# Dilated-window attention and MLP, two layers on one core: chunk products added on DVE, weights spread by DMA, stages reordered, first layernorm transposed on PE

## The chip, the cores, the metric

The kernel runs on 1 core of a Trainium2 chip. The metric is device time in microseconds (us), median of several executions. Engines: PE does the matmuls, DVE is the vector engine, ACT the scalar engine, POOL is GpSimd, SP issues most of the DMAs. Most executions of one kernel agree within about 0.3% (1350.36 to 1353.33 us before the change). Some fall into a slower state, and are not compared. They show a lower granted PE clock: the share of PE's full speed that the chip allowed, 1.00 being all of it.

## The reference

```python
def _A_ref(x, wqkv, wo):            # H = 32 heads of 32, window W = 8, dilation 2
    qkv = x @ wqkv                  # S = 2048, D = 1024
    # position s attends to s, s-2, ..., s-14 (masked where negative)
    logits = einsum("bhsd,bhswd->bhsw", q, kg) * Dh ** -0.5
    attn = softmax(where(mask, logits, -1e9), axis=-1)
    o = einsum("bhsw,bhswd->bhsd", attn, vg)
    return o.reshape(B, S, D) @ wo

def _B_ref(x, w1, b1, w2, b2):      # F = 3584
    return gelu(x @ w1 + b1) @ w2 + b2

x = A_x
for layer in range(2):              # written out in the original
    x = x + _A_ref(_layernorm(x), A_wqkv, A_wo)
    x = x + _B_ref(_layernorm(x), B_w1, B_b1, B_w2, B_b2)
```

All in bf16, with f32 sums in PSUM.

## The kernel before

The sequence is cut into 4 groups of 512 positions; with 2 layers that makes 8 units of work, "groups 0 to 7". A group passes the stages qkv (24 chunks of 8 matmuls, 128x128 weights against 512 columns), wo (8 chunks), ffn1 (28 chunks of 8) and ffn2 (32 rows of 7): 704 main matmuls. The attention sits between them on DVE, with PE helping in two places: the head sums (sum of q*k over the 32 values of a head, by a 0/1 matrix) and the spread of the attention weights from 32 rows per block to 128 partitions.

Names in the profiles: `wt` is a tile of weights, `xn` the layernorm of x and `xnT` its transpose, `qT`, `kT` and `vT` the outputs of qkv, `big` a product on DVE, `L` the head sums, `a` the attention weights and `abc` the same after the spread, `oT` the output of the attention, `hT` that of ffn1, `tmp` a step of the sum into x, and `acc` a buffer in PSUM, where the matmuls write. "av" multiplies the spread weights by v and adds over the window.

```python
wpool = ctx.enter_context(tc.tile_pool(name="wpool", bufs=6))   # 1 MB weight tiles
...
def mm(*args, **kwargs):                  # PE keeps the order of the program
    inst = nc.tensor.matmul(*args, **kwargs)
    if last_pe[0] is not None:
        dep_order(inst, last_pe[0], "PE program order")
    ...
def ln_tile(t, tt, xnT):
    ...                                   # bn_stats, bn_aggr on DVE, rstd on POOL
    nc.vector.tensor_scalar(out=xn[:], in0=x[t][:], scalar1=mv[:, 0:1], scalar2=rstd[:], ...)
    nc.sync.dma_start_transpose(xnT[:, tt, :, :], xn[:].rearrange("s (k p) -> s k p", p=P))

def gen_qkv(n):
    ...
    def reduce_one():                     # head sum of one chunk: 8 matmuls on PE
        c, prod = pend.pop(0)
        for wh in range(2):
            for tb in range(NTT):
                mm(L[tb*H:(tb+1)*H, wh*4:(wh+1)*4, :], lhsT=smat[:], rhs=prod[...],
                   start=(c == 0), stop=(c == NCH - 1), tile_position=(0, tb * H))
        if c == NCH - 1:
            ...                           # mask
            softmax(s, L)
    for c in range(NCH):                  # k chunks
        ps = qkv_chunk(wk, c, xnT)
        nc.scalar.copy(kT[:, c, HALO:], ps[:])
        nc.vector.tensor_tensor(out=prod[:], in0=qT[...], in1=win(kT[:, c, :]), op=ALU.mult)
        pend.append((c, prod))
        if len(pend) > 2:
            reduce_one()
    ...                                   # v chunks, with the last reduce_one()s

def spread(n):                            # 8 matmuls and 8 ACT copies
    for wh in range(2):
        for tb in range(NTT):
            mm(ps[:], lhsT=selbc[...], rhs=a[...], tile_position=(tb * H, 0))
            nc.scalar.copy(abc[...], ps[...])

def av(n, c):                             # one chunk: multiply, then add over the window
    nc.vector.tensor_tensor(out=pv[:], in0=abc, in1=win(vT[:, c, :]), op=ALU.mult)
    ...                                   # three adds, 2048, 1024 and 512 columns

# order of the stages
mk_ln_a(0); run(gen_qkv(0), ...)
run(gen_qkv(1), {1: spread(0), 2 + c: av(0, c), 12: layernorm of 2})
run(gen_wo(0))
for n in range(1, N):
    run(gen_ffn1(n - 1), {1: spread(n), 2 + 3 * c: av(n, c)})
    # last n: wo(n), ffn2(n-1), ffn1(n), ffn2(n); otherwise:
    run(gen_ffn2(n - 1), {8: layernorm of n + 1}); run(gen_wo(n)); run(gen_qkv(n + 1))
```

## Time and profile before

| | before |
|---|---|
| time, median of 4 | 1351.88 us |
| span of the profile | 1350.7 us |
| PE busy | 1285.6 us, 95% |
| head-sum matmuls on PE | 512 |
| first main matmul | 24.8 us |

The first fence is the page of the kernel before; the columns of an engine are busy us, share of the span, and number of instructions.

```profile
span 1350.7 us, 14693 instructions
PE 1285.6 (95%) x6222; PEld 628.1 (46%) x6222; DVE 722.0 (53%) x809; ACT 329.3 (24%) x530; POOL 56.0 (4%) x158
```

PE is the bound, but 95% busy doesn't say what a busy microsecond does. The chain of waits of the same kernel does (start in us, duration in us, engine, what it wrote, source line, number of instructions):

```profile
340.38 0.69 ACT hT L308
341.07 1.46 ACT abc L261 x3
342.57 126.21 PE acc L87 x584
468.77 0.55 PE L L87 x8
469.32 1.88 PE acc L87 x8
471.20 0.55 PE L L87 x8
...
500.31 0.69 ACT hT L308
```

584 matmuls in 126.21 us are 216.1 ns each. From one head-sum block to the next (468.77 to 471.20) 2.43 us pass, while 8 main matmuls need 1.73 us: a block costs PE 0.70 us, though it shows as 0.55. From 340.38 to 500.31 one group takes 159.93 us; its 704 main matmuls need 152.1.

What PE itself waited for, all of the run (engine, line, releaser: us in total, times, longest):

```profile
PE acc L87 <- DMA xnT<-xn: 31.8, 2, 24.8
PE L L87 <- DVE big L220: 24.6, 4, 14.7
PE acc L87 <- ACT hT L308: 1.7, 7, 0.2
```

All the large waits lie before 183 us. The timeline shows the one at the start (start, duration, engine, operation, count; in brackets the idle time before it and its releaser):

```profile
10.03 6.10 SPq L151 DMA_TRANSPOSE xnT<-xn  x2
18.17 4.50 SPq L151 DMA_TRANSPOSE xnT<-xn  x2
24.78 20.77 PE L87 MATMUL acc<-xnT,wt 128*128 128x512 bf16 x88 [24.78 <-DMA xnT<-xn]
```

And a window (start:end, length, then busy us of each engine, then the granted PE clock) shows PE starved by DVE in the av chain of group 0, with the clock down:

```profile
115.00:130.00 15.00, 7.51 (x40) 2.86 (x39) 15.00 (x12) 1.17 (x2) 0.00 (x0) 0.73 0.00 0
```

DVE is busy for all of the 15 us, PE for half of them, at a clock of 0.73.

### The profile page before, as it was taken

The numbers are of one execution on the slowest core, as the hardware profiler recorded it, in microseconds if no ns is written. First come the engines' busy times: TensorE is split into PE (matmuls) and PEld (weight loads), VectorE is DVE, ScalarE is ACT, GpSimd is POOL, SyncE is SP. The second block draws the span as 40 slices with busy tenths as digits, with TensorE's granted clock in tenths as the row PEclk, the third lists the DMA queues.
The fourth block names the chain that finished last, engine by engine and source line by source line (L and its number), as shares of the span: only waits on it lengthen the run. The fifth ranks groups of instructions, "written<-read, shape, count | busy, mean of one in ns | idle before, by whom it ended". The sixth has DMA issues, their size and how long they took to land.

```text
span 1350.7 us, 14693 instructions
## 1 busy us (share of the span) xinstructions
PE 1285.6 (95%) x6222; PEld 628.1 (46%) x6222; DVE 722.0 (53%) x809; ACT 329.3 (24%) x530; POOL 56.0 (4%) x158
## 2 busy tenths in 40 slices
PE   2893979999999999999999999999999999999998
PEld 1461534455444554445544454445544455444443
DVE  3669754177723759147571666417782455932003
ACT  1240233013520254102540035201441024400310
POOL 3100000010000100001000100001000000000000
PEclk9896989999999999999999999999999999999999
DMA  9740554554645544555645545456464654466440
GB/s 257 212 163 15 157 145 139 168 156 126 197 145 169 174 140 148 155 159 147 183 140 175 166 147 171 145 170 178 132 183 145 206 167 127 147 173 198 154 137 31
DMA packets 218976, 210.93 MB, mean 156 GB/s; under 512 B 71392, under 2 KB 190176, under 8 KB 216864
## 3 DMA queue, kind: packets, MB, share of 16 engines
q1 hardware_dynamic: 218752, 209.74, 51.3%
q8 instruction: 48, 0.79, 0.2%
q0 software_dynamic: 160, 0.27, 0.2%
q14 instruction: 16, 0.13, 0.0%
HBM read 189.01 MB, written 4.19 MB: 143 GB/s over the span
## 4 chain that ended last, share of the span: by engine, by line
PE 90%; DVE 4%; ACT 2%; DMA 1%; issue 0%; POOL 0%; SPq 0%; DVEq 0%; ACTq 0%
PE acc L87 87%; PE L L87 3%; DVE big L268 1%; ACT abc L261 1%; DVE big L269 1%; DVE big L220 0%; DVE stats L143 0%; DMA xnT<-xn 0%; ACT hT L308 0%; DVE big L270 0%; DMA x_93<-in_A_x_dram 0%; DVE xn L150 0%; SPq L151 0%; POOL rstd L148 0%; DVE oT L271 0%
## 5 line engine op out<-in xcount | busy, mean ns | idle before, releaser
L87 PE MATMUL acc<-xnT,wt 128*128 128x512 bf16 x3328 | 743.0, 383 | 32.7 <-DMA xnT<-xn 31.8
L87 PEld LDWEIGHTS <-wt 128*128 128x128 bf16 x3328 | 391.5, 120 | 383.4 <-issue 67.0
L87 PE MATMUL acc<-wt,hT 128*128 128x512 bf16 x1792 | 388.1, 379 | 0.0
L87 PEld LDWEIGHTS <-hT 128*128 128x128 bf16 x1792 | 175.3, 98 | 211.4
L327 DVE TENSOR_TENSOR tmp<-acc,b2bc 128x512 f32<-128x512 f32 x64 | 44.3, 692 | 393.9 <-PE acc L87 389.5
L308 ACT ACTIVATE hT<-acc,b1T 128x512 bf16<-128x512 f32 x224 | 154.3, 690 | 285.2 <-PE acc L87 285.1
L220 DVE TENSOR_TENSOR big<-qT,kT 128x4096 bf16<-128x4096 bf16 x64 | 143.0, 2286 | 44.6 <-ACT kT L218 43.7
L268 DVE TENSOR_TENSOR big<-abc,vT 128x4096 bf16<-128x4096 bf16 x64 | 143.7, 2285 | 28.9 <-ACT abc L261 28.9
L194 ACT CAST qT<-acc 128x512 bf16<-128x512 f32 x64 | 37.6, 587 | 465.3 <-PE acc L87 465.3
L87 PE MATMUL acc<-wt,oT 128*128 128x512 bf16 x512 | 111.8, 379 | 0.0
L87 PEld LDWEIGHTS <-oT 128*128 128x128 bf16 x512 | 50.1, 98 | 60.3
L269 DVE TENSOR_TENSOR big<-big 128x2048 bf16<-128x2048 bf16 x64 | 75.4, 1218 | 0.0
L218 ACT CAST kT<-acc 128x512 bf16<-128x512 f32 x64 | 37.5, 586 | 132.4 <-PE acc L87 132.4
L87 PE MATMUL L<-big,smat 128*32 128x512 bf16 x512 | 41.2, 399 | 24.6 <-DVE big L220 24.6
L147 POOL TENSOR_TENSOR rstd<-mv,eps_t 128x1 f32<-128x1 f32 x64 | 14.6, 231 | 1143.5 <-DVE mv L145 1143.5
L232 ACT CAST vT<-acc 128x512 bf16<-128x512 f32 x64 | 37.4, 584 | 70.0 <-PE acc L87 69.8
L270 DVE TENSOR_TENSOR big<-big 128x1024 bf16<-128x1024 bf16 x64 | 41.3, 685 | 0.0
L148 POOL TENSOR_TENSOR rstd<-rstd,mhalf 128x1 f32<-128x1 f32 x64 | 35.7, 561 | 4.1
L261 ACT CAST abc<-acc 128x512 bf16<-128x512 f32 x64 | 32.0, 629 | 0.0
L87 PEld LDWEIGHTS <-smat 128*32 128x32 bf16 x512 | 8.2, 95 | 49.7 <-issue 49.7
L241 DVE TENSOR_REDUCE mx<-L 128x128 f32<-128x1024 f32 x8 | 9.7, 1218 | 29.9 <-PE L L87 29.9
L246 DVE TENSOR_REDUCE z<-e 128x128 f32<-128x1024 f32 x8 | 15.7, 1964 | 16.5 <-ACT e L244 16.5
(102 smaller groups left out, 331.6 us busy)
## 6 DMA issues: line engine op xcount, KB each, us to landing
wt<-in_B_w_dram SPq DMA_DIRECT2D x56, 1024.0 KB, 5.6
wt<-in_B_w_dram SPq DMA_DIRECT2D x64, 896.0 KB, 4.8
wt<-in_A_wqkv_dram SPq DMA_DIRECT2D x48, 1024.0 KB, 5.4
wt<-in_A_wo_dram SPq DMA_DIRECT2D x16, 1024.0 KB, 4.9
xnT<-xn SPq DMA_TRANSPOSE x64, 4.2
x_85<-in_A_x_dram SPq DMA_DIRECT2D x1, 256.0 KB, 2.8
x_86<-in_A_x_dram SPq DMA_DIRECT2D x1, 256.0 KB, 3.1
x_87<-in_A_x_dram SPq DMA_DIRECT2D x1, 256.0 KB, 4.1
```

Of the source, the lines that this page charges most:

```text
L87: inst = nc.tensor.matmul(*args, **kwargs)
L148: nc.gpsimd.tensor_tensor(out=rstd[:], in0=rstd[:], in1=mhalf[:], op=ALU.pow)
L194: nc.scalar.copy(qT[:, c, :], ps[:])
L218: nc.scalar.copy(kT[:, c, HALO:], ps[:])
L220: nc.vector.tensor_tensor(out=prod[:], in0=qT[:, c, :].unsqueeze(1).to_broadcast([P, W, T]), in1=win(kT[:, c, :]), op=ALU.mult)
L232: nc.scalar.copy(vT[:, c, HALO:], ps[:])
L261: nc.scalar.copy(abc[:, wh * 4:(wh + 1) * 4, tb * P:(tb + 1) * P], ps[:].rearrange("p (w t) -> p w t", w=4))
L268: nc.vector.tensor_tensor(out=pv[:], in0=s["abc"][:], in1=win(s["vT"][:, c, :]), op=ALU.mult)
L269: nc.vector.tensor_tensor(out=pv[:, 0:4, :], in0=pv[:, 0:4, :], in1=pv[:, 4:8, :], op=ALU.add)
L270: nc.vector.tensor_tensor(out=pv[:, 0:2, :], in0=pv[:, 0:2, :], in1=pv[:, 2:4, :], op=ALU.add)
L308: nc.scalar.activation(hT[:, j, :], ps[:], ACT.Gelu_apprx_tanh, bias=b1T[:, j:j + 1])
L327: nc.vector.tensor_tensor(out=tmp[:], in0=pss[tt][:], in1=b2bc[:, dh * HALF:(dh + 1) * HALF], op=ALU.add)
```

## The change

The intent is to leave PE only main matmuls, and to keep it fed from the start on:

1. In groups 2 to 7, the 8 products are added on DVE (7 adds in a tree), and PE sums heads once instead of 8 times. The head sum moved into `attend`, 5 chunks into the following ffn1.
2. In groups 2 to 6 the weights are spread by DMA through DRAM: 4 DMAs out, 4 back.
3. The first layernorm is transposed on PE, with warm-up matmuls around it.
4. qkv(1) and two thirds of qkv(2) come ahead of wo(0), and the wo stages of groups 1 and 7 are put inside ffn2 of the group before, after 4 of its 32 rows. The layernorms of groups 1 and 2 are scaled on ACT.

To pay for the memory there are 5 weight buffers instead of 6. Smaller changes go with it: the order of instructions is pinned on POOL, and on DVE in the first layernorm; x and the weights are loaded in another order; the constants are built later; and the first six q chunks of qkv(0) run in two halves, so that they can start with half of the weights.

```diff
-    wpool = ctx.enter_context(tc.tile_pool(name="wpool", bufs=6))
+    wpool = ctx.enter_context(tc.tile_pool(name="wpool", bufs=5))
+    dram = ctx.enter_context(tc.tile_pool(name="dram", bufs=2, space=bass.MemoryType.DRAM))
...
+    vec, act, pool, sp = InOrder(nc.vector), InOrder(nc.scalar), InOrder(nc.gpsimd), InOrder(nc.sync)
...
+    def ln_first():
+        ...
+            for k in range(KD):
+                pe(nc.tensor.transpose(pst[:, k, :], xn[:, k * P:(k + 1) * P], ident[:]))
+            act.copy(xa[0][:, tt, :, :], pst[:])
+            warm_up(4)
...
+    def new_prod(n, c):
+        vec.tensor_tensor(out=prod[:], in0=qT..., in1=win(kT...), op=ALU.mult)
+        tree.append(prod)
+        if s["on_pe"]:
+            if len(tree) > 2:
+                head_sum(n, tree.pop(0), False)
+        elif c % 2 == 1:
+            for _ in range(min(2, len(tree) - 1)):
+                b = tree.pop()
+                vec.tensor_tensor(out=tree[-1][:], in0=tree[-1][:], in1=b[:], op=ALU.add)
...
+        if on_pe:
+            ...                                   # as before
+            return
+        a_d = dram.tile([H, W, T], BF16, name="a_d")
+        for tb in range(NTT):
+            pool.dma_start(a_d[:, :, tb * P:(tb + 1) * P], a[tb * H:(tb + 1) * H, :, :])
+        for j in range(HP):
+            pool.dma_start(abc[j::HP, :, :], a_d[:, :, :])
...
+    pool.on = True                                # POOL keeps the order of the program
+    warm_up(16)
+    ln_first()
+    stage(gen_qkv(0, sum_on_pe=True), sides=at(0, load_x, 1) + at(2, ln_a, 1, True) + ... + at(18, attend, 0))
+    with tc.tile_pool(name="early", bufs=1) as early:
+        q1 = gen_qkv(1, sum_on_pe=True, defer=True, qk_pool=early)
+        stage(q1, sides=at(0, ln2) + at(1, spread, 0, True) + each(av, 0, 2, 1))
+        q2 = gen_qkv(2, defer=True)
+        stage(q2, 16, sides=each(new_prod, 1, 2, 1.5))
+        stage(gen_wo(0), sides=at(1, attend, 1))
+        stage(q2, sides=at(2, spread, 1, True) + each(av, 1, 3, 1))
+    stage(gen_ffn1(0), sides=each(new_prod, 2, 20, 1))
+    f2 = gen_ffn2(0)
+    stage(f2, 4)
+    stage(gen_wo(1))
+    stage(f2, sides=at(2, attend, 2) + at(2, spread, 2))
+    stage(gen_ffn1(1), sides=each(av, 2, 1, 2))
+    stage(gen_ffn2(1), sides=at(2, ln_a, 3))
+    for n in range(2, N - 1):
+        stage(gen_wo(n))
+        stage(gen_qkv(n + 1))
+        last = n + 2 == N
+        stage(gen_ffn1(n), sides=at(4, attend, n + 1) + at(9 if last else 4, spread, n + 1, last) + each(av, n + 1, 9, 2))
+        f2 = gen_ffn2(n)
+        ...   # not last: rest of ffn2 with the layernorm of n+2; last: 4 rows, wo(n+1), rest
```

## The prediction

> **What bounds it now.** The tensor engine (PE). Page: PE busy 1285.6 of 1350.7 us; chain of waits: 90% PE. The chain has uninterrupted stretches of 584 matmuls in 126.21 us, 216.1 ns each (the Trainium skill, "TensorE: Matmul & The Clock Gate", Part 1, gives 215.7 ns warm; the trace agrees). The 5632 main 512-column matmuls need 1217 us at that rate and are untouched. So about 134 us can be won:
>
> - first main matmul at 24.8 us (timeline: DMA transposes of the first layernorm queue behind weight loads);
> - head sums: in the chain 8 blocks of 8 matmuls plus their restarts cost 5.4 us per group, 43 us over 8 groups, 0.68 us a block;
> - spreading weights on PE: steady groups are 159.9 us apart, 704 matmuls need 152.1, minus 5.4 leaves 2.4 us a spread, 19 us in all;
> - waits before 183 us (waits of PE): 24.6 on DVE products, 31.8 on xnT (24.8 of it the start), plus perhaps 10 us of lowered clock after them (granted clock 0.71 to 0.88 in those windows);
> - tail 4 us.
>
> **The change, costed.**
> 1. Groups 2 to 7 sum chunk products on DVE: 56 of 64 head-sum matmuls go, 7x0.68 = 4.8 us each, -29 us. DVE gains 7 adds of 128x4096 bf16, 2.2 to 2.3 us each (the multiply of that size takes 2286 ns; "VectorE: DVE Perf Modes", tier table, caps two-tensor bf16 ops at 2x, which that fits): +95 us, 722 to about 815 us, off the critical path. Products plus tree take 33 us, from about 16 us into qkv; the head sum comes at about 50 us: it just fits, at most 1 us of wait.
> 2. Five spreads by DMA: -12 us of PE, -25 us of ACT. Price is latency (two hops, my estimate 15 us), hidden under ffn1/ffn2, with only some 3 us of slack before av delays the first ffn2 evictions.
> 3. PE transposes at the start: last x tile lands near 7 us, DVE layernorm done near 12, PSUM copy about 1 us: first main matmul near 14 us, -10.5 us.
> 4. New order: qkv(1), most of qkv(2) between av(0) and wo(0) hide the 36.9 us DVE chain that starved PE between 84 and 130 us: most of the 32 us of waits and 10 us of clock go.
>
> Ideal sum: 14.3 + 1217 + 11 (groups 0, 1) + 4 + 7 (three PE spreads) + 4 = 1257.5.
>
> **Given back.** In the built instruction order the SP queue blocks with five weight buffers: transposes of layernorm 2 wait until qkv(0) releases its v weights, which delays the ACT copies of spread(0), about 4 us; the second wo(0) tile can load only when k of group 2 ends, 4 us; transposes for ffn1(0) stand behind a w1 load waiting for the end of v, about 11 us plus 1.5 us of clock; products behind layernorm(1), 2 us; the two wo stages placed within ffn2 have two PSUM buffers only, 3 us. Later waits, 2 us. Together 28.
>
> **Prediction: 1285 us, 8 in 10 between 1265 and 1305.** Faster by over 2%: 0.96; within 2%: 0.035; slower: 0.005.
>
> **Right if** the head-sum group falls from 512 to about 176 matmuls, DVE busy is about 815 us, steady groups are about 153 us apart, the first main matmul comes at 13 to 16 us, and remaining PE waits name xnT (ffn1(0)) and wt/abc in the first 200 us. **Wrong** if steady groups exceed 155 us: then the head sum waits for the DVE tree or av waits for the abc DMA; or if no xnT wait stands before ffn1(0) (then near 1265).
>
> **What would make it wrong:** DMA spreads far slower than 15 us beside weight loads; fewer weight buffers starving PE; my hand placement of the early waits, which is the least certain term.

## The result, and the profile after

| | before | after |
|---|---|---|
| time, median | 1351.88 us (1350.36 to 1353.33) | 1280.68 us (1279.91 to 1281.26) |
| span of the profile | 1350.7 us | 1278.2 us |
| PE busy | 95% | 98% |
| DVE busy | 722.0 us | 808.3 us |
| head-sum matmuls | 512 | 176 |
| first main matmul | 24.8 us | 13.8 us |
| one steady group | 159.9 us | 152.9 us |

The ratio is 0.9473, 95% interval 0.9457 to 0.9489. A ratio here is the mean time of one kernel's fast runs over that of the other's of the same rounds, so not quite the ratio of the medians. Both kernels are correct.

The page of the changed kernel:

```profile
span 1278.2 us, 14116 instructions
PE 1252.9 (98%) x5861; PEld 630.7 (49%) x5910; DVE 808.3 (63%) x843; ACT 322.4 (25%) x502; POOL 85.0 (7%) x217
```

In this trace most lines carry L93 or L115, since every operation goes through a wrapper that keeps order; one goes by what is written and read. The timeline of PE alone:

```profile
13.77 19.15 PE L115 MATMUL acc<-xnT,wt 128*128 128x512 bf16 x88 [0.34 <-ACT xnT L93]
407.90 50.24 PE L115 MATMUL acc<-xnT,wt 128*128 128x512 bf16 x232
458.37 0.62 PE L115 MATMUL L<-big,smat 128*32 128x512 bf16 x8 [0.24 <-DVE big L93]
560.80 50.24 PE L115 MATMUL acc<-xnT,wt 128*128 128x512 bf16 x232
611.28 0.61 PE L115 MATMUL L<-big,smat 128*32 128x512 bf16 x8 [0.24 <-DVE big L93]
```

A qkv stage starts every 152.90 us (407.90, 560.80); 152.1 are main matmuls. In each steady group there is one head-sum block left, and PE waits 0.24 us ahead of it: the tree of adds on DVE ends almost exactly when PE arrives. The chain of waits of the changed kernel says the same in another way:

```profile
423.64 0.59 ACT kT L93
424.25 8.91 DVE big L93 x4
...
456.03 2.30 DVE big L93
458.37 0.62 PE L L115 x8
458.99 40.03 PE acc L115 x185
```

From the first k chunk (424.25) to the head sum the chain runs over DVE, 34.1 us for 15 operations, although PE was busy nearly all of that time. A chain names the last releaser, even when it was last by 0.24 us. So "PE 75%, DVE 18%" of the chain does not mean that DVE costs 18%; it means that there is no slack left on that side.

What PE waited for:

```profile
PE L L115 <- DVE big L93: 3.7, 6, 2.5
PE acc L115 <- DMA wt<-in_A_wo_dram: 3.3, 1, 3.3
PE acc L115 <- ACT abc L93: 2.7, 2, 2.4
PE acc L115 <- DVE x_91 L93: 2.3, 1, 2.3
PE acc L115 <- ACT qT L93: 1.7, 2, 1.4
```

The 58 us of waits before became 17. There is no line for xnT any more: neither at the start, nor ahead of ffn1(0), where the prediction had put 11 us.

The DMA spread, in the timelines of POOL and DVE for group 3. Weights `a` are written at 466.87, the first av operation reads `abc` at 478.88:

```profile
468.39 2.35 POOL L93 DMA_DIRECT2D a_d<-a  x4 [56.11 <-DVE a L93]
472.92 2.08 POOL L93 DMA_DIRECT2D abc<-a_d  x4 [2.18 <-DMA a_d<-a]
```

```profile
466.87 1.22 DVE L93 TENSOR_TENSOR a<-e,z 128x1024 bf16<-128x1024 f32 x1
478.88 4.50 DVE L93 TENSOR_TENSOR big<-abc,vT 128x4096 bf16<-128x4096 bf16 x2 [1.21 <-DMA abc<-a_d]
```

From the end of `a` (468.09) to the landing of `abc` the two hops took 10.8 us, against 15 estimated (the prediction doesn't say from what).

Last, the region that was predicted wrongly. SP issues the w1 loads and the transposes for ffn1(0):

```profile
165.31 0.38 SPq L93 DMA_DIRECT2D wt<-in_B_w_dram  x1
166.81 5.22 SPq L93 DMA_TRANSPOSE xnT<-xn  x2
```

and PE in wo(1), which runs between row 4 and row 5 of ffn2(0):

```profile
236.48 3.62 PE L115 MATMUL acc<-wt,oT 128*128 128x512 bf16 x16
242.39 2.84 PE L115 MATMUL acc<-wt,oT 128*128 128x512 bf16 x7 [2.30 <-DVE x_91 L93]
245.45 9.14 PE L115 MATMUL acc<-wt,oT 128*128 128x512 bf16 x40 [0.22 <-issue]
254.44 4.70 PE L115 MATMUL acc<-wt,hT 128*128 128x512 bf16 x20
```

The w1 load left at 165.31, as wo(0) ended, not at 182 as v ended. And wo(1) took 18.0 us (236.48 to 254.44) for 64 matmuls that need 13.8. Four of the six PSUM buffers were held by ffn2(0); the other two were full, and DVE freed the first (x_91) only behind most of the product tree of group 2. The waits are 2.5 of the 4.1 us lost; the rest is the clock, which was 0.61 after the gap and then 0.50 until 246 us.

### The profile page after: what moved, and what is told of

Same layout as the page of the kernel before. It is cut to its first block, busy times and chain, and to the rows that moved or that the text cites. A ratio compares the mean times of both kernels' runs of the same rounds, so it can differ in the third digit from the quotient of the medians.

```text
span 1278.2 us, 14116 instructions
## 1 busy us (share of the span) xinstructions
PE 1252.9 (98%) x5861; PEld 630.7 (49%) x5910; DVE 808.3 (63%) x843; ACT 322.4 (25%) x502; POOL 85.0 (7%) x217
## 4 chain that ended last, share of the span: by engine, by line
PE 75%; DVE 18%; issue 2%; ACT 2%; DMA 2%; SPq 0%; POOL 0%; DVEq 0%; ACTq 0%; POOLq 0%
PE acc L115 74%; DVE big L93 17%; DMA x_91<-in_A_x_dram 1%; PE L L115 1%; ACT abc L93 1%; ACT xn L93 0%; DVE z L93 0%; DVE stats L93 0%; DMA wt<-in_A_wo_dram 0%; DMA xnT<-xn 0%; SPq L93 0%; ACT kT L93 0%; ACT qT L93 0%; DVE oT L93 0%; DVE a L93 0%
## 5 line engine op out<-in xcount | busy, mean ns | idle before, releaser
L115 PE MATMUL acc<-xnT,wt 128*128 128x512 bf16 x3328 | 728.3, 381 | 3.0 <-ACT abc L93 2.4
L115 PEld LDWEIGHTS <-wt 128*128 128x128 bf16 x3328 | 395.3, 119 | 334.3 <-issue 17.4
L115 PE MATMUL acc<-wt,hT 128*128 128x512 bf16 x1752 | 386.5, 379 | 2.1
L115 PEld LDWEIGHTS <-hT 128*128 128x128 bf16 x1792 | 175.2, 98 | 211.7 <-issue 0.4
L93 ACT ACTIVATE hT<-acc,b1T 128x512 bf16<-128x512 f32 x224 | 152.7, 687 | 266.4 <-PE acc L115 265.7
L93 DVE TENSOR_TENSOR tmp<-acc,b2bc 128x512 f32<-128x512 f32 x64 | 44.2, 690 | 271.8 <-PE acc L115 269.0
L93 DVE TENSOR_TENSOR big<-big 128x1024 bf16<-128x1024 bf16 (+2 forms) x170 | 209.9, 1279 | 1.2
L93 DVE TENSOR_TENSOR big<-qT,kT 128x4096 bf16<-128x4096 bf16 x64 | 143.6, 2286 | 63.7 <-ACT kT L93 54.4
L93 DVE TENSOR_TENSOR big<-abc,vT 128x4096 bf16<-128x4096 bf16 x64 | 143.5, 2282 | 22.3 <-ACT abc L93 15.3
L93 ACT CAST qT<-acc 128x512 bf16<-128x512 f32 x64 | 37.0, 585 | 373.7 <-PE acc L115 373.7
L115 PE MATMUL acc<-wt,oT 128*128 128x512 bf16 x503 | 115.0, 387 | 6.2 <-DMA wt<-in_A_wo_dram 3.3
L115 PEld LDWEIGHTS <-oT 128*128 128x128 bf16 x512 | 50.8, 99 | 69.0 <-issue 11.2
L93 POOL TENSOR_TENSOR rstd<-mv,eps_t 128x1 f32<-128x1 f32 x64 | 12.8, 201 | 792.0 <-DVE mv L93 791.1
L93 ACT CAST kT<-acc 128x512 bf16<-128x512 f32 x64 | 37.3, 587 | 78.0 <-PE acc L115 78.0
L93 ACT CAST vT<-acc 128x512 bf16<-128x512 f32 x64 | 37.6, 588 | 76.2 <-PE acc L115 76.2
L93 POOL TENSOR_TENSOR rstd<-rstd,mhalf 128x1 f32<-128x1 f32 x64 | 38.4, 601 | 5.0
L93 POOL DMA_DIRECT2D a_d<-a x20 | 11.8, 615 | 235.6 <-DVE a L93 235.6
L93 ACT ACT_TABLE_LOAD x14 | 18.0, 1283 | 35.1 <-PE acc L115 34.1
L93 DVE TENSOR_REDUCE z<-e 128x128 f32<-128x1024 f32 x8 | 15.3, 1915 | 13.8 <-ACT e L93 13.8
L93 DVE TENSOR_TENSOR oT<-big 128x512 bf16<-128x512 bf16 x64 | 24.0, 413 | 0.0
L93 ACT ACTIVATE e<-e 128x1024 f32<-128x1024 f32 x8 | 8.5, 1058 | 34.8 <-DVE e L93 34.7
L115 PE MATMUL L<-big,smat 128*32 128x512 bf16 x176 | 13.2, 384 | 3.7 <-DVE big L93 3.7
```

Of the source, the lines that this page charges most:

```text
L93: inst = f(*args, **kwargs)
L115: return pe(nc.tensor.matmul(*args, **kwargs))
```

## The experiments

Each experiment changes the changed kernel, and each time stands beside runs of the kernel before on the same chip, whose medians were 1350.85 to 1352.52 us. All gave correct results. "+" and "-" below are differences of medians to 1280.68 us, so across jobs; they are good to a microsecond or two (by the ratios, e6 comes to -5 and e9 to -4). The runs of e6 (1272.53 to 1275.40) and of e9 (1273.61 to 1277.89) lie wholly below those of the changed kernel (1279.91 to 1281.26).

| run | time, us | ratio to before | difference to the changed kernel |
|---|---|---|---|
| e1_sums_on_pe | 1301.93 | 0.9629 | +21 |
| e2_spread_on_pe | 1348.46 | 0.9978 | +68 |
| e2b_spread_pe_u9 | 1301.20 | 0.9633 | +21 |
| e3_ln_dma | 1287.77 | 0.9520 | +7 |
| e4_old_start | 1306.91 | 0.9664 | +26 |
| e5_attend_u2 | 1306.37 | 0.9673 | +26 |
| e6_late_v | 1274.81 | 0.9436 | -6 |
| e8_spread01_dma | 1294.30 | 0.9584 | +14 |
| e8b_spread_first | 1285.59 (fast runs) | 0.9510 | +5 |
| e8b_again | 1285.01 | 0.9496 | +4 |
| e9_split16 | 1276.15 | 0.9444 | -5 |
| b2_all | 1260.24 | 0.9329 | -20 |

### Part 1 undone: head sums on PE (e1_sums_on_pe)

```diff
-        s["on_pe"] = sum_on_pe
+        s["on_pe"] = True
```

> The changed kernel with one part undone: every group sums its chunk products on PE. Theory (each block of 8 head-sum matmuls costs PE 0.68 us, restart of the main matmuls included): 42 blocks come back, +28.6 us, less about 1.2 us of the five 0.24 us waits for the DVE tree, so 1306 to 1310 us; steady groups 157.5 us apart instead of 152.9; DVE busy about 712 us. Rival A (a block costs only its streaming, 0.55 us): +22 us. Rival B (the tree merely moved PE's work to a wait on DVE, gain elsewhere): under +5 us.

It took 1301.93 us, +21: below the range of the theory, and 1 us under the 1303 of rival A. The time alone doesn't separate the two, but the trace does, in the distance between two qkv stages (the second line is cut off by the window of the view):

```profile
408.05 19.16 PE L115 MATMUL acc<-xnT,wt 128*128 128x512 bf16 x88
565.28 15.06 PE L115 MATMUL acc<-xnT,wt 128*128 128x512 bf16 x69
```

Steady groups are 157.2 us apart, +4.3 each, which for seven more blocks and 0.24 us less wait is 0.65 us a block: between the theory's 0.68 and the rival's 0.55. Five such groups make 21.7, about the whole difference, and the theory had counted six. So group 2 gives nothing: its 7 extra blocks cost PE 4.5 us in this run, but qkv(3) starts at 408.05 us, against 407.90 in the changed kernel. In the changed kernel the tree of group 2 delays the wo stage of group 1 (18.0 us); in this run that stage took 13.8 us (240.34 to 254.16). The tree's gain and its cost in that place cancel. Rival B (the gain is elsewhere) falls.

### Part 2 undone, twice: spreads on PE

```diff
-        if on_pe:
+        if True:
             for wh in range(2):
```

> One part undone: all eight spreads on PE and ACT again. Theory: five spreads at 2.4 us, +12 us; the ones for groups 3 to 6 now come at the same place as the head sum, before the weights are ready, so PE waits there for the softmax as well: up to 8 us each more, that is 1292 us if the placement costs nothing and up to 1325 us if PE waits for the softmax (the spread stands right behind the head sum in PE order). Rival (PE pays nothing, since spreads overlap): 1281 us.

1348.46 us, far above the expectation. PE waits, in this run:

```profile
PE acc L115 <- DVE a L93: 44.8, 6, 11.7
```

PE stood at the spread, which came right behind the head sum, while the softmax ran. The waits were about as expected (8.2 us in group 3, 11.7 in group 2), but the clock fell behind them: it was 0.50 from 487.3 to 492 us, behind that wait, and 0.970 over the run, against 0.993. This tells what a wrong place costs, not what a spread costs, so it was done again with the spread put 5 chunks behind the head sum:

```diff
-        stage(gen_ffn1(n), sides=at(4, attend, n + 1) + at(9 if last else 4, spread, n + 1, last) + ...
+        stage(gen_ffn1(n), sides=at(4, attend, n + 1) + at(9, spread, n + 1, True) + ...
-    stage(f2, sides=at(2, attend, 2) + at(2, spread, 2))
+    stage(f2, sides=at(2, attend, 2) + at(9, spread, 2, True))
```

> The spread part undone again, now with the PE spreads of groups 2 to 6 put where the changed kernel has the one of group 7: five chunks of ffn1 behind the head sum (nine rows of ffn2 for group 2), so that the softmax has about 9 us. Theory (a PE spread costs 2.4 us of PE, and the first attempt's 45 us of waits came from its place alone): +12 us for five spreads plus about 1 us each of remaining wait, 1293 to 1299 us; waits of PE for the weights a at most 6 us in all. Rival (DMA spreads are worth far more than 2.4 us each): above 1305 us.

1301.20 us, +21, above the expected 12 to 18 and below the rival's 1305. Steady groups are 155.5 us apart (qkv starts at 416.41 and 571.95), +2.6 each and +4.3 in the last: the 2.4 us a spread of the prediction, nearly. The rest lies in group 2, whose spread had to go into ffn2(0) and cost 8.5 us there (ffn1(1) starts at 305.91 instead of 297.39), with waits for `a` (2.5 us), for DVE and for ACT. So the DMA spread is worth 2.6 us in a steady group, and more in group 2 only because PE has no good place for it.

### Part 3 undone: first layernorm through DMA transposes (e3_ln_dma)

```diff
-            pst = psum.tile([P, KD, P], BF16, name="acc", bufs=6)
-            for k in range(KD):
-                pe(nc.tensor.transpose(pst[:, k, :], xn[:, k * P:(k + 1) * P], ident[:]))
-            act.copy(xa[0][:, tt, :, :], pst[:])
-            warm_up(4)
+            sp.dma_start_transpose(xa[0][:, tt, :, :], xn[:].rearrange("s (k p) -> s k p", p=P))
```

> One part undone: the first layernorm goes through DMA transposes again. Theory: first main matmul at 22 to 25 us instead of 13.8, +8 to +11 us, 1289 to 1292 us, nothing absorbed later. Rival (the start is absorbed, because the DVE chain of groups 1 and 2 ends at 242 us on its own schedule): less than +3 us.

1287.77 us (1283.59 to 1289.88), +7. The first main matmul came at 19.45 us, not at 22 to 25. So of the 11 us won at the start, the transposes account for 5.7. The edit also took out the warm-up matmuls between them, and the first 88 main matmuls took 20.62 us instead of 19.15 (clock 0.50 up to 22 us). The profiled run is the fastest of the four, only 3.7 us above the profile of the changed kernel; but it runs 5.6 us behind as far as qkv(7) (1025.39 against 1019.78 us), and only there does the changed kernel lose 1.7 us to the clock (0.53 from 1083 to 1086 us) that this run doesn't. So the loss at the start is not absorbed, and the rival falls. The other 5.3 us must lie in what this run kept, such as the pinned order on DVE, or the issue order of weights and x. Which of them was not tried.

### Part 4 undone: old order at the start (e4_old_start)

```diff
+    stage(gen_qkv(1, sum_on_pe=True), sides=at(1, spread, 0, True) + each(av, 0, 2, 1) + at(12, ln_a, 2, True) + at(18, attend, 1))
+    stage(gen_wo(0))
+    stage(gen_ffn1(0), sides=at(1, spread, 1, True) + each(av, 1, 2, 3))
+    stage(gen_ffn2(0))
-    ...                                # the new order of these stages
-    for n in range(2, N - 1):
+    for n in range(1, N - 1):
```

> One part undone: the old order of the stages for groups 0 and 1 (qkv0, qkv1 with its products at once, wo0, ffn1 of 0 with av of 1, ffn2 of 0, then the steady loop from group 1), the rest as changed. Theory: the PE waits on DVE products (24.6 us before) and on xnT ahead of ffn1 (7.0 us), with about 10 us of lowered clock, come back, less the 9 us of waits that the new order has: +25 to +35 us, 1305 to 1315 us. Rival (the order bought little, the waits went with the head sums): under +10 us.

1306.91 us, +26. PE waits:

```profile
PE L L115 <- DVE big L93: 22.2, 9, 14.7
PE acc L115 <- DMA xnT<-xn: 7.3, 1, 7.3
```

PE again waits 22.2 us in all for DVE products, 14.7 of it at once at 109 us, and 7.3 us for xnT ahead of ffn1(0): nearly the same waits as in the kernel before, although parts 1 to 3 are in place. The theory stands. One wait of this run, 8.7 us at the first head sum, is its own (2.5 us in the changed kernel). The edit also dropped `ln2`, which holds the layernorm of group 2 back on DVE: here DVE takes its statistics from 29.61 us on, and the first product begins at 40.25 us instead of 33.10. Without this wait the order would be worth some 20 us.

The four undone parts give 21 + 21 + 7 + 26 = 75 us, where the whole change gives 71: they nearly add. The 4 us between are within what four such differences can be off by, and e4's own wait would explain them too. So the smaller changes, which all these runs kept, have little left to give in sum; that says nothing of each alone.

### No slack behind the tree: head sum two chunks earlier (e5_attend_u2)

```diff
-        stage(gen_ffn1(n), sides=at(4, attend, n + 1) + ...
+        stage(gen_ffn1(n), sides=at(2, attend, n + 1) + ...
```

> Only the place of the head sum of groups 3 to 7 changes: after 3 chunks of ffn1 instead of 5, 3.46 us earlier. Theory (the DVE product tree ends 0.24 us after PE arrives, so there is no slack at all): each of the five waits grows from 0.24 to 3.7 us, +17 us, plus up to 1 us of lowered clock each: 1296 to 1304 us. Rival (the tree has slack, the 0.24 us is only the semaphore): waits stay under 1 us each and the time stays within 3 us of 1281.

1306.37 us, +26, above the upper end. The waits are as the theory says, 3.69 us each. The timeline of PE, and a window behind such a wait:

```profile
460.68 1.05 PE L115 MATMUL L<-big,smat 128*32 128x512 bf16 x8 [3.69 <-DVE big L93]
```

```profile
462.00:464.00 2.00, 2.00 (x6) 0.76 (x5) 1.97 (x2) 0.00 (x0) 0.00 (x0) 0.50 0.03 8
```

The granted clock is 0.50 for some 5 us behind the wait: 6 matmuls in 2 us instead of 9. Groups are 159.3 us apart instead of 152.9, +6.4, of which the wait is 3.45 and the clock nearly all of the rest. So the head sum can stand 5 chunks into ffn1 at next to no cost, as it can one chunk later (b2_all), but 3 chunks is too early, and missing the place by 3.5 us costs nearly double. 4 chunks were not run.

### Late v weights (e6_late_v)

```diff
-        wv = load_qkv(2)
+        if n != 2:
+            wv = load_qkv(2)          # ahead of the k chunks
...
+        if n == 2:
+            wv = load_qkv(2)          # behind them
```

> The v weights of group 2 are loaded behind its k stage, so that the two wo weights for group 0 find buffers earlier. Theory: the 3.3 us wait for the wo weight and about 1.6 us of lowered clock behind it vanish, -4 to -5 us, since the DVE chain behind it (softmax of group 1, av of 1, products of 2) starts earlier by the same: 1276 to 1277 us. Rival (PE then arrives earlier at the wo stage of group 1 and waits longer there for DVE): less than 1.5 us gained, wait for x at that stage grows from 2.3 to 5 us or more.

1274.81 us, -6. The wait for the wo weight is gone, and the stage wo(1) waits 3.5 us for DVE in all (2.3 before): the DVE chain starts earlier with PE, as the theory said. The rival falls.

### The two early spreads by DMA too (e8_spread01_dma, e8b_spread_first, e8b_again)

```diff
-        stage(q1, sides=at(0, ln2) + at(1, spread, 0, True) + each(av, 0, 2, 1))
+        stage(q1, sides=at(0, ln2) + at(1, spread, 0) + each(av, 0, 2, 1))
-        stage(q2, sides=at(2, spread, 1, True) + each(av, 1, 3, 1))
+        stage(q2, sides=at(2, spread, 1) + each(av, 1, 3, 1))
```

> The two early spreads (groups 0 and 1) go by DMA too. Measured in the changed kernel for group 3: 10.8 us from the end of the weights to the landing of the spread, while the PE way of group 1 took from 165.1 to 175.9 us, so latency is equal. Theory: PE gains 2 x 2.4 us and loses the 4.1 us of waits on ACT around the first spread, -7 to -9 us: 1272 to 1274 us. Rival (the DVE chain of groups 1 and 2, without slack at the wo stage of group 1, absorbs it): -0 to -4 us, with a wait for x at that wo stage above 4 us.

1294.30 us, +14: against both. Less work on PE and ACT made it slower. The spread of group 0 landed 23.6 us after its weights, not 10.8, and a likely reason is that POOL keeps the order of its program, where the layernorm of group 2 came first. PE then waited 10.8 us at head sums and 14.5 us for x in wo(1). To test that, the two were swapped:

```diff
-        stage(q1, sides=at(0, ln2) + at(1, spread, 0) + each(av, 0, 2, 1))
+        stage(q1, sides=at(0, spread, 0) + at(1, ln2) + each(av, 0, 2, 1))
```

> As the run with both early spreads by DMA, but the DMA spread of group 0 is issued ahead of the layernorm of group 2 in the program order of GpSimd. There the spread left 7.2 us after its weights were ready, behind that layernorm, and landed 23.6 us after them, so av of group 0 began at 87.5 us instead of 75. Theory (the DVE chain of groups 0 to 2 bounds everything up to the wo stage of group 1, and that order alone delayed it): av of group 0 begins at 73 to 77 us again, the waits for DVE at the head sum and at wo shrink to under 6 us together, time 1274 to 1281 us. Rival (DMA spreads are slow in the early phase in themselves, beside weight loads and transposes): av still begins after 82 us and the time stays above 1287 us.

1285.59 us for the three fast runs: 9 better than without the swap, short of the 1274 to 1281 expected. The profiled execution fell in the slow state (1383 us, clock 0.916), so its waits prove nothing:

> The same kernel as the run before with the spread ahead of the layernorm, since its profile fell in the slow state (clock 0.916) and can't be compared. Expected of a fast profile: av of group 0 begins near 78 us (the slow one: 80.4), about 14 us after its weights, so the order in GpSimd's program was the cause of the late spread; the rest of the loss is a new wait of PE for the ACT copies of k in group 1 (20.2 us in the slow profile), because ACT stands at a layernorm tile of group 2 whose statistics now come behind av of group 0 on DVE; time 1283 to 1287 us. If that wait is under 5 us in the fast profile, the loss lies elsewhere.

1285.01 us, with a fast profile. Half of the expectation held: av of group 0 begins at 78.56 us instead of 87.47, so the order on POOL was the main cause in group 0. The spread still lands 14.9 us after its weights, not 10.8. The other half fell: there is no wait for ACT copies of k at all; that 20 us wait was of the slow execution alone. What remains is 14.6 us of waits for x in wo(1), and the timelines of POOL and DVE show their source, in group 1, whose weights were written at 156.7 us:

```profile
164.69 2.52 POOL L93 DMA_DIRECT2D a_d<-a  x4
172.67 2.11 POOL L93 DMA_DIRECT2D abc<-a_d  x4 [5.46 <-DMA a_d<-a]
```

```profile
181.52 4.49 DVE L93 TENSOR_TENSOR big<-abc,vT 128x4096 bf16<-128x4096 bf16 x2 [16.20 <-DMA abc<-a_d]
```

The same thing again one group later: the first DMA leaves 8 us after its weights, as soon as POOL is through with the layernorm of group 0 in wo(0), and the spread lands 24.8 us after them. In the changed kernel the PE way took 10.8 us there (165.1 to 175.9). DVE stood idle for 16.2 us, and PE waits for DVE later. The transfers themselves are slower too: from issue to landing 5.4 us for an `a_d` and 6.8 for an `abc` (median), against 2.1 and 4.2 in group 3 of the changed kernel, with the DMA engines busy for 88% or more of each stretch between 164 and 182 us. So "equal latency", which the expectation took from group 3, doesn't hold where POOL has other work in front and the DMA engines are full.

### wo of group 1 after 16 rows (e9_split16)

```diff
     f2 = gen_ffn2(0)
-    stage(f2, 4)
+    stage(f2, 16)
     stage(gen_wo(1))
```

> Only one number changes: the wo stage of group 1 comes after 16 rows of ffn2 of group 0 instead of 4, so it has all six PSUM buffers and 18 us more for the DVE chain. Theory (that stage took 18.0 us instead of 13.8, as it waited for a PSUM buffer that DVE frees only behind the product tree of group 2): -4 us, 1276 to 1277 us, no wait for x there. Rival (the lost time comes back in ffn1 of group 1, whose spread and av start 18 us later): no gain, new waits for tmp or oT.

1276.15 us, -5, as the theory said.

```profile
254.63 13.98 PE L115 MATMUL acc<-wt,oT 128*128 128x512 bf16 x63
```

wo(1) takes 13.8 us (254.63 to 268.44) and waits for nothing. One number repairs what the tree of group 2 had cost.

### All together (b2_all)

```diff
+    # late v weights (e6); spreads of 0 and 1 by DMA, 0 ahead of the layernorm (e8b); stage(f2, 16) twice (e9)
-        ... at(4, attend, n + 1) + at(9 if last else 4, spread, n + 1, last) + ...
+        ... at(5, attend, n + 1) + at(5, spread, n + 1) + ...
+        if n == 0:
+            load_x(1)                 # ahead of the k weights, instead of at(0, load_x, 1)
```

> What the runs point to, together: v weights of group 2 loaded late (-6), all spreads by DMA with group 0's ahead of the layernorm (-2 to -7 beyond the lost last PE spread, -3), wo of groups 1 and 7 after 16 rows of ffn2 (-4), head sum one chunk later (-1), x of group 1 loaded ahead of the k weights (-2). If the savings add: 1258 to 1264 us, floor by the main matmuls 1217 + start 14 + tail 4 + head sums 15 = 1250. If the early DVE chain absorbs them: about 1270 us.

1260.24 us (1257.98 to 1261.74), ratio to before 0.9329 (0.9311 to 0.9346), the best of all, within the expected range. What PE still waits for:

```profile
PE L L115 <- DVE big L93: 3.5, 1, 3.5
PE acc L115 <- DVE tmp L93: 1.6, 1, 1.6
PE acc L115 <- DVE big L93: 1.0, 1, 1.0
```

The 0.24 us waits are gone. Loading x earlier bought nothing visible: the first head sum waits 3.5 us instead of 2.5. The spread of group 1 is as late as before (24.7 us; av of group 1 begins at 178.0 us), but PE waits only 1.6 us in wo(1) instead of 14.6. That fits the 18 us by which wo(1) comes later; no run shows it apart from the other changes.

## Why the prediction was right or wrong

The time, 1280.68 us, lies within 1265 to 1305 and 4.3 us below the centre. Its marks came out as named (176 matmuls, 808 us of DVE, 152.9 us, 13.8 us, waits for wt and abc), but for one: no wait for xnT stands before ffn1(0). The prediction had called that a mark of being wrong, with a time near 1265. So part of the closeness is luck: 12.5 us of the 28 given back did not occur, and some 5 us elsewhere took their place. Point by point:

- **The bound and the rate.** Right. 216.1 ns a main matmul before, and 152.9 us for a group of 704 after.
- **Head sums, "-29 us".** Mis-sized. Per steady group 4.3 us were measured by undoing it, and 4.8 credited; and group 2 brought nothing in the changed kernel, because its tree stands in front of wo(1) on DVE. It is 21 us by the run with head sums on PE.
- **"It just fits, at most 1 us of wait".** Right: 0.24 us, five times. Moving the head sum 3.46 us earlier made the waits 3.69 us, so there was indeed no slack.
- **Spreads by DMA, "-12 us" with a latency of 15 us.** Right for the steady groups: 2.6 us each and 10.8 us of latency. Undoing it costs 21 us, since group 2 loses 8.5.
- **Start, "-10.5 us".** Right in size: 24.8 to 13.8 us. Only 5.7 of the 11 come from the transposes themselves.
- **New order, "most of the 32 us of waits and 10 us of clock go".** Right: undone, 26 us come back, with the old waits by name.
- **"Given back: 28 us".** The list was right in its small terms: the wo weight 3.3 us (4 predicted; its removal brought 5 to 6, with the clock), ACT copies of the first spread 4.1 us (1.43 + 0.30 + 2.37; 4 predicted), products behind layernorm(1) 2.5 us (2), later waits about 2 us (2). One term failed.

The step that failed: "transposes for ffn1(0) stand behind a w1 load waiting for the end of v, about 11 us plus 1.5 us of clock". That wait did not exist. I had assumed that the five weight buffers are taken in fixed rotation, so that this load would need the buffer of the v weights. The trace shows it leaving at 165.31 us, when wo(0) ended, and the transposes right behind it; so it took the buffer of a wo weight: those of the v weights were in use until 182 us. In the same stretch a smaller loss was under-sized: wo(1) lost 4.1 us alone, where 3 were given for it and its twin in group 7. The twin lost none (13.8 us).

The sum of the terms as measured is 1257.5 (ideal) + 2.5 + 4.1 + 3.3 + 1.6 + 4.1 + 2 = 1275 us of span; 1278.2 were measured. Two stretches of lowered clock that no term holds are enough for the remaining 3 us: 224 matmuls from 73.48 us, behind the first spread, took 51.17 us where as many take 48.5 later (clock 0.50 to 0.52 until 79 us), and the 1.7 us from 1083 us on.

## What to carry to other kernels

When PE is the bound, cost a helper matmul by the distance between two of them in the chain, not by its own bar: 0.70 us against 0.55. Here moving work off PE was free only where the receiver had slack at that place (groups 3 to 7, but not group 2). So look for the place where the moved work ends just ahead of its reader, and move the reader, as one number (4 rows or 16) was worth as much as a whole group's head sums. A DMA replaced a compute step well here where it left at once and found the DMA engines free: on an engine that keeps program order, look at what stands in front of it.

## What the Trainium skill lacked or had wrong

- "TensorE: Matmul & The Clock Gate", the table "Why this matters for your kernels", asks for no PE-idle gaps above about 3 us. Here a gap of 2.3 us (240.1 to 242.4 us, changed kernel) was followed by a clock of 0.61 and then 0.50 until 246 us, while one of 2.52 us at 33 us was followed by 1.00. The page's Part 1 says that the window runs freely, which would fit, but its rule is too mild as a limit. Behind 3.69 us (e5_attend_u2) the clock was 0.50 for some 5 us. And behind two waits of 0.43 and 0.34 us, close together, it was 0.53 from 1083 to 1086 us in the changed kernel, while it stayed 1.00 behind the same two waits in e3_ln_dma.
- "TensorEngine Tiling (Array Packing)", Key Properties, says that a change of tiling mode drains the engine, without a size. In these traces a block of 8 tiled matmuls (four column tiles, two rounds) between full ones took 0.55 us and lengthened the restart by 0.15 us.
- "DMA: Bandwidth & Descriptors", the anatomy of a DMA issued from GpSimd, gives about 2.0 us plus the bytes over 436 GB/s. The runs agree for 64 KB (2.1 us from issue to landing, median, in group 3 of the changed kernel). The 256 KB of the second hop took 4.2 us, where the formula gives about 2.6 as an estimate; four of them were in flight together. The two hops of a spread took 10.8 to 24.8 us; of the 14 us between, about 8 were the wait on GpSimd in front of the first issue and about 6 the slower transfers (5.4 and 6.8 us). The page has nothing on what a chain of two DMAs through DRAM takes.
- No page says how freed buffers of a tile pool are handed out; the failed step of the prediction rested on a guess of fixed rotation, and the w1 load at 165.31 us shows otherwise.
